# Sigmoid attention and a gated feed-forward network: the last four f chunks of batch 1 as a third unit of seven products

## The chip, the cores and the metric

The kernel runs on one core of one Trainium2 chip, in one launch. The metric is device time in microseconds; three runs of the kernel before gave 387.45, 387.88 and 389.07, a median of 387.88. One more execution was profiled.

Engines are named as in the profile: PE is TensorE (PEld its weight loads), DVE is VectorE, ACT is ScalarE, POOL is GpSimd, SP is SyncE.

## The reference

```python
# q, k, v: (8, 12, 448, 64) float32; w_gate, w_val: (768, 1536); w_out: (1536, 768)
scores = q @ k.T / sqrt(64) - log(448)
attn   = 1 / (1 + exp(-scores))                  # a sigmoid, no row sums
x      = (attn @ v), heads side by side          # (8 * 448, 768)
out    = (max(x @ w_gate, 0) * (x @ w_val)) @ w_out
```

## The kernel before

**Tiles.** All matmuls take 16-bit operands. A batch has 448 tokens and 12 heads; heads go in six pairs (the 768 model columns as six slices of 128), and three groups of four heads, g = 0, 1, 2. The 1536 hidden columns are twelve f chunks of 128. The 448 keys are seven chunks c of 64. A *scores unit* (b, g, c) (`qk_unit`) is eight matmuls of 64x64x448, four at a time in the four quadrants of TensorE, into two PSUM banks, and two sigmoids on ScalarE (L187) into a tile PT. A *PV* (`pv_group`) multiplies the seven PT tiles of a group by v into two banks, which VectorE empties into xT (L184). xT is x transposed, one tile a batch.

**PSUM.** Eight banks in a ring, `free`. `bank()` takes the next one; `later()` moves some to the back. A bank is written again when its reader is done.

**Feed-forward units.** For a plain chunk, `gv` makes gate and value products of one f chunk (twelve matmuls, L322), ScalarE or VectorE takes the positive part, VectorE multiplies into hT (L343). Batch 0 is done in two halves of 256 and 192 tokens (`push_first`, `ffn_mix`), between the scores of batch 1.

`gv_split(b, f)` (kind `"s"`) does four f chunks of one batch at once. It cuts the problem into 2x2 blocks (two halves of the model columns; gate and value weights; two halves of the tokens) and uses seven block products instead of eight, each twelve matmuls of 128x128x224 (L718). It needs sums of the weights: S3 = gate - value in place of half of the value weights (`gate_sums`), S2, S1, S4 (`unit_sum_steps`), each 128x768 on VectorE, for each pair of f chunks; and sums of the tokens T1, T2, T4, T3 (`split_sums`). From batch 2 on, two batches are taken together in the same scheme (`gv_pair`, kind `"w"`), with sums X of the tokens.

The last product with w_out is done in pairs of token tiles, `down_pair(g, p)` (kind `"y"`), seven products of six matmuls 128x128x384 (L389), with sums T of w_out (`weight_sums(i)`, 128x2304 each, one in place), sums S of hT (`token_sum_steps`), and results added up in `ysb`. For pairs in `SUMS_LATE` the product A12 x B21 comes second and has bank `a` of its own from the start; for others `a` is taken after the scores units that `amid` puts into the middle.

**Order.** It is written out by hand. `order` lists the 21 scores units of a batch; `cuts` cuts them into bursts, `pv_at` puts PVs into them. Batch b's loop runs burst, work, burst, work: for b = 1 the work is `ffn_mix(mix[m])` half-chunks of batch 0, from b = 2 on it is `next_work`, which pops the deque `work`. For b = 2 this is `("u", 1, 8), ("s", 1, 0), ("u", 1, 9), ("s", 1, 4), ("u", 1, 10), ("u", 1, 11)`, where `"u"` is a plain chunk of 448 tokens. `ahead` runs before a unit's matmuls are recorded, `jobs` in its middle (`beside`).

**Loads and transposes.** GpSimd issues all loads, in order; each issue waits until the one eight before it has landed. k and q of batch 0 and 1 are transposed on TensorE; from batch 2 on `dma_transposes(b, g)` copies k and q of a group into a tile `rel` (two 128x896 copies on VectorE, L222), and SP issues a DMA transpose into `qkT` (three buffers). `rel` has two buffers. `hold` is a copy on GpSimd that reads a transposed tile, so that the loads behind it (`late_loads`: v of batch 2, k and q of batch 3, w_out) wait for transpose (2, 1).

Of the kernel before, what the change touches and what calls it, by code (L numbers as in the profile page):

```python
# [18 lines left out]
def kernel(  # L19
# [75 lines left out]
    def tiles_of(b):  # L95
        if b not in in_tiles:
            pool = early if b == 1 else inp
# [58 lines left out]
    load(1, 1, 2, "kq")  # L156
    load_gv(6, 9)
    load_v(1)
    load(1, 2, 3, "kq")
    load_gv(9, 12)  # L160

# [55 lines left out]

    def dma_transposes(b, g):
        k16, q16, _ = in_tiles[b]
        rel = relp.tile([P, TW, P], FP16, tag="rel", name="rel")  # L220
        for ti, t16 in enumerate((k16, q16)):
            nc.vector.tensor_copy(  # L222
                rel[:, ti * NCH : (ti + 1) * NCH, :].rearrange("p c (h d) -> p h c d", h=2),
                t16[:, 2 * g : 2 * g + 2, :].rearrange("p h (c d) -> p h c d", c=NCH),
            )
        nc.sync.dma_start_transpose(
            qkT_of(b, g)[:], rel[:].rearrange("p c x -> p (c x)")
        )

    def row_of(r, hh):  # L230
# [139 lines left out]
    def open_late():  # L370
        first_sbuf.close()
        pool = ctx.enter_context(tc.tile_pool(name="late", bufs=1))
        T = pool.tile([P, 3, HF, HM], FP16, tag="T", name="T")
        late["T"] = [T[:, 0], T[:, 1], wo[:, 0:HF, HM:DM], T[:, 2]]
        late["odd"] = pool.tile([P, NFC, P], FP16, tag="odd", name="odd")
        late["X"] = pool.tile([P, 3, HD, S], FP16, tag="X", name="X")
        late["sums"] = ctx.enter_context(tc.tile_pool(name="sums", bufs=2))

    def sub(o, a, b):
# [26 lines left out]
    FRESH = {1: 0, 2: 0, 3: NPP}  # L406
    SUMS_LATE = {(1, 0), (1, 1), (2, 0), (2, 1), (3, NPP)}
    odd = {}
# [150 lines left out]

    def early_sum_steps(j, f):  # L560
        views = []
        for i in range(3 * j, 3 * j + 3):
            t = early.tile([P, 2, 512], FP16, tag=f"PT{i}", name="S")
            flat = t[:].rearrange("p a y -> p (a y)")[:, 0 : HD * 2 * P]
            views.append(flat.rearrange("p (x y) -> p x y", y=2 * P))
        yield lambda: gate_sums(f, f + 2)
        yield from unit_sum_steps(("s", f), f, views)

    def unit_sum_steps(key, f, tiles):
# [3 lines left out]
        S3, A22 = wv[:, 0:HD, fs], wv[:, HD:NDC, fs]  # L573
        sums[key] = S1, S2, S4
        return (
            lambda: sub(S2, A22, S3),
            lambda: nc.vector.tensor_tensor(out=S1, in0=S2, in1=A11, op=AOP.add),
            lambda: sub(S4, A12, S2),
        )

    def batch_blocks(g, ks):
        x1, x2 = xT_tiles[2 * g], xT_tiles[2 * g + 1]
        lo, hi = slice(*ks), slice(HD + ks[0], HD + ks[1])
        return [late["X"][:, i, lo] for i in range(3)] + [x1[:, lo], x1[:, hi], x2[:, lo], x2[:, hi]]

# [12 lines left out]
    def gv_pair(g, f, beside, first_copy):  # L598
        x1, x2 = xT_tiles[2 * g], xT_tiles[2 * g + 1]
        T1, T2, T4 = (late["X"][:, i] for i in range(3))  # L600
        B11, B21, T3, B22 = x1[:, 0:HD], x1[:, HD:NDC], x2[:, 0:HD], x2[:, HD:NDC]
# [82 lines left out]
    def split_sums(b):  # L684
        tile_ = xTp.tile([P, NPAIR, S], FP16, tag="xT", name="X2")
# [7 lines left out]
        sub(T1, B12, B11)  # L693
        sub(T2, B22, T1)
        sub(T4, B21, T2)
        sub(T3, B22, B12)

    def gv_split(b, f, beside):
# [8 lines left out]
        for j in range(4):  # L707
            us, fs = slice(j % 2 * P, (j % 2 + 1) * P), slice((f + j) * P, (f + j + 1) * P)
            S1, S2, S4 = (t[:, :, us] for t in sums[("s", f + j // 2 * 2)])
            sets.append((  # L710
                wg[:, 0:HD, fs], wg[:, HD:NDC, fs], wv[:, HD:NDC, fs],
                S1, S2, wv[:, 0:HD, fs], S4,
            ))
# [151 lines left out]

    def hold(b, g):
        nc.gpsimd.tensor_copy(gate[0:1, :], qkT_tiles[(b, g)][0:1, 0, 0:2])

# [39 lines left out]
    def next_work(jobs=(), alone=False, amid=None, ahead=()):  # L908
# [11 lines left out]
        if kind == "y":  # L920
            down_pair(g, i, beside, prepare, not work, scaled_act if alone else scaled, amid)
        elif amid:
# [11 lines left out]
    for b in range(1, B):  # L934
        if b == 1:
            cuts, pv_at = (0, 3, 6, 9, 13, 17, 21), {3: (0, 2), 5: (1, 2)}
        else:
            cuts, pv_at = (0, 4, 7, 11, 14, 18, 21), {0: (-1, 2), 2: (0, 2), 4: (1, 2)}
        bursts = list(range(len(cuts) - 1))
# [7 lines left out]
        if b == 1:  # L947
            mix = (4, 3, 3, 3, 3, 4)
            hooks = {
                1: [(3, lambda: both(1, 1))],  # L950
                3: [(3, lambda: both(1, 2))],
                4: [(2, lambda: dma_transposes(2, 0)), (0, lambda: dma_transposes(2, 1))],
                5: [(4, late_loads)],
            }
            steps = itertools.chain.from_iterable(early_sum_steps(j, 2 * j) for j in range(4))
            given = ((0, 0, 1, 1, 1), (0, 1, 1, 1), (0, 1, 1, 1), (0, 1, 1, 0), (2, 0, 0, 0), (0, 1, 1, 1, 0))
        else:
            mix = (0,) * count

        def burst(n):  # L960
            for i, (g, c) in enumerate(order[cuts[n] : cuts[n + 1]]):
# [9 lines left out]
                qk_unit(b, g, c)  # L971

        for m in range(count):
# [22 lines left out]
            if b == 2 and m == 0:  # L996
                ahead.append(lambda: split_sums(1))
            elif b == 2 and m == 4:
                open_late()
                first_sums = token_sum_steps(0, 0)  # L1000
                ahead += [*first_sums[:2], lambda: weight_sums(0)]
            elif b == 2 and m == 5:
                ahead += [lambda: weight_sums(1), lambda: dma_transposes(3, 2)]
                jobs += first_sums[2:]
            elif b == 3 and m == 0:
                jobs.append(lambda: (weight_sums(2), weight_sums(3)))
            elif b == 3:
                jobs.append(lambda: gate_sums(6 + 2 * m, 8 + 2 * m))
                if m == 1:
                    jobs.append(lambda: keep_odd(0))  # L1010
# [55 lines left out]
```

## Time and profile before

| | us |
|---|---|
| median of three runs | 387.88 |
| profiled execution | 388.3 |
| its span, first to last instruction | 386.5 |
| PE busy | 381.1 |
| DVE busy | 304.9 |
| ACT busy | 227.3 |
| POOL busy | 49.8 |
| granted TensorE clock, mean | 0.999 |

The page's second part gives the load of the DMA engines in 40 slices of 9.7 us; it is nine tenths or more in the first eleven slices and mostly lower after them. Matmuls are pipelined and a group's end is modelled, so durations of neighbours on PE overlap; the difference of two starts is what a group took.

Stages, from TensorE's order of time: first slots of batch 0 up to 29.70; batch 1's scores between batch 0's half-chunks up to 61.30; batch 2's scores between batch 1's feed-forward units up to 95.81; from there on batch 3's scores between the first pairs of the output product, in steps of 9.9 us.

### The profile page before, as it was taken

Reading aid. Unit: us, or ns where it says so; the run is one execution under the profiler, and the core shown is the slowest. Engines: PE = TensorE matmul, PEld = TensorE weight load, DVE = VectorE, ACT = ScalarE, POOL = GpSimd, SP = SyncE. Lnnn points to the kernel's source line nnn. Section 1 sums busy time; section 2 is a strip of 40 time slices with the busy share of each in tenths; the row PEclk is TensorE's granted clock in tenths of the full one; section 3 lists DMA queues with packets and bytes.
Section 4 is the critical chain, followed back from the end, with each engine's and each line's share of the span. In section 5 each row is a group of like instructions: output and inputs, shape, how many; then the busy total and the mean of one; then the engine's idle time right before and its main releaser. Section 6 shows DMA issues by size and latency. Waiting matters only on the chain.

```text
span 386.5 us, 8978 instructions
## 1 busy us (share of the span) xinstructions
PE 381.1 (99%) x3570; PEld 223.2 (58%) x3570; DVE 304.9 (79%) x611; ACT 227.3 (59%) x480; POOL 49.8 (13%) x73
## 2 busy tenths in 40 slices
PE   8999999999999999999999999999999999999996
PEld 6678776885555545455555554545455555555654
DVE  3455667769868999999868789999978788999653
ACT  5967887567777645455777764545477344333322
POOL 8643306100400003000300300000000000000000
PEclk9999999999999999999999999999999999999999
DMA  9999999999979302952499893222013220000235
GB/s 171 199 199 204 204 193 161 208 208 135 179 168 178 81 2 37 182 95 47 43 229 220 171 233 56 44 54 50 0 28 76 72 75 0 2 0 0 73 92 165
DMA packets 67563, 43.81 MB, mean 113 GB/s; under 512 B 35648, under 2 KB 64192, under 8 KB 67520
## 3 DMA queue, kind: packets, MB, share of 16 engines
q0 software_dynamic: 28960, 23.24, 39.2%
q1 hardware_dynamic: 37792, 19.34, 24.5%
q10 hardware_dynamic: 768, 0.66, 0.6%
q8 instruction: 28, 0.46, 0.5%
q14 instruction: 15, 0.12, 0.1%
HBM read 47.19 MB, written 11.01 MB: 151 GB/s over the span
## 4 chain that ended last, share of the span: by engine, by line
PE 96%; ACT 2%; DMA 1%; DVE 0%; issue 0%
PE u L389 34%; PE g L389 16%; PE y L389 12%; PE qk_ps L239 10%; PE pv_ps L257 8%; PE g_ps L322 5%; PE v_ps L322 5%; PE u L718 2%; PE g L718 2%; ACT PT L187 2%; DMA qkT<-rel 1%; PE warm_ps L175 1%; PE trt L204 1%; DVE ysb L544 0%; DVE zeros L130 0%
## 5 line engine op out<-in xcount | busy, mean ns | idle before, releaser
L187 ACT ACTIVATE PT<-qk_ps 128x448 f16<-128x448 f32 (+3 forms) x318 | 150.9, 584 | 79.2 <-PE qk_ps L239 79.1
L389 PEld LDWEIGHTS <-S 128*128 128x128 f16 x576 | 56.3, 98 | 45.9
L628 DVE TENSOR_TENSOR gsb<-g,gsb 128x448 f32<-128x448 f32 x72 | 42.7, 623 | 7.9 <-PE g L389 7.5
L239 PE MATMUL qk_ps<-qkT 64*64 64x448 f16 (+2 forms) x756 | 47.5, 337 | 0.7 <-DMA qkT<-rel 0.3
L389 PEld LDWEIGHTS <-hT 128*128 128x128 f16 x318 | 29.5, 98 | 24.0 <-issue 6.1
L257 PE MATMUL pv_ps<-PT,v 64*64 64x448 f16 (+2 forms) x756 | 36.6, 329 | 0.0
L468 DVE SCALAR_TENSOR_TENSOR ysb<-y,ysb 128x384 f32<-128x384 f32 x33 | 18.3, 555 | 20.7 <-PE y L389 14.1
L184 DVE TENSOR_SCALAR xT<-pv_ps 128x448 f16<-128x448 f32 (+2 forms) x53 | 27.8, 566 | 8.0 <-PE pv_ps L257 6.9
L389 PEld LDWEIGHTS <-wg 128*128 128x128 f16 x216 | 20.2, 98 | 21.8 <-issue 4.3
L389 PEld LDWEIGHTS <-wv 128*128 128x128 f16 x216 | 21.1, 98 | 19.7
L450 ACT ACTIVATE ysb<-u 128x384 f32<-128x384 f32 x28 | 13.8, 491 | 30.9 <-PE u L389 26.8
L389 PE MATMUL u<-wo,hT 128*128 128x384 f16 x156 | 29.8, 327 | 0.0
L239 PEld LDWEIGHTS <-qkT 64*64 64x64 f16 x756 | 17.6, 106 | 21.0 <-issue 14.1
L111 POOL DMA_DIRECT2D k<-in_k_dram x14 | 10.8, 775 | 141.0 <-DVE rel L222 135.9
L257 PEld LDWEIGHTS <-v 64*64 64x64 f16 x756 | 21.4, 107 | 11.1 <-issue 0.5
L389 PE MATMUL u<-xT,wg 128*128 128x448 f16 x108 | 23.5, 354 | 0.0
L389 PE MATMUL u<-xT,wv 128*128 128x448 f16 x108 | 23.4, 352 | 0.0
L389 PE MATMUL g<-X,S 128*128 128x448 f16 x108 | 23.4, 352 | 0.0
L389 PE MATMUL u<-X,S 128*128 128x448 f16 x108 | 23.4, 352 | 0.0
L389 PE MATMUL g<-xT,S 128*128 128x448 f16 x108 | 23.4, 352 | 0.0
L389 PE MATMUL g<-xT,wg 128*128 128x448 f16 x108 | 23.4, 352 | 0.0
L389 PE MATMUL u<-X,wv 128*128 128x448 f16 x108 | 23.4, 352 | 0.0
(98 smaller groups left out, 563.9 us busy)
## 6 DMA issues: line engine op xcount, KB each, us to landing
out_dram<-ysb SPq DMA_DIRECT2D x53, 192.0 KB, 3.1
v<-in_v_dram POOLq DMA_DIRECT2D x8, 336.0 KB, 15.3
v<-in_v_dram POOLq DMA_DIRECT2D x16, 168.0 KB, 15.1
k<-in_k_dram POOLq DMA_DIRECT2D x4, 672.0 KB, 11.6
q<-in_q_dram POOLq DMA_DIRECT2D x4, 672.0 KB, 14.8
wo<-in_moe_w_out_dram POOLq DMA_DIRECT2D x2, 1152.0 KB, 19.2
k<-in_k_dram POOLq DMA_DIRECT2D x9, 224.0 KB, 11.8
q<-in_q_dram POOLq DMA_DIRECT2D x7, 224.0 KB, 12.3
```

The source lines that it names most:

```text
L111: nc.gpsimd.dma_start(t16[:, xs, cs], rows_of(src, b)[:, xs, cs])
L175: nc.tensor.matmul(ps[:, 0:n], zeros[:, 0:P], zeros[:, 0:n], start=True, stop=True)
L184: nc.vector.tensor_scalar(out=xT, in0=src, scalar1=XSCALE, scalar2=None, op0=AOP.mult)
L187: nc.scalar.activation(PT_ap, ps_ap, AF.Sigmoid, bias=sig_bias, scale=qk_scale)
L239: nc.tensor.matmul(out_of(hh)[o : o + 64, :], qkT[rows, c, cols], qkT[rows, NCH + c0 : NCH + c1, cols], start=True, stop=True, tile_positi ...
L257: nc.tensor.matmul(ps[hh][64 * r : 64 * r + 64, 0:qn], v16[rows, 2 * g + hh, c * D : (c + 1) * D], pieces[c][rows, hh, :], start=(c == 0), ...
L322: nc.tensor.matmul(ps[:, 0:qn], (wg, wv)[i][:, dc, f * P : (f + 1) * P], xT_tiles[b][:, dc, q0 : q0 + qn], start=(dc == 0), stop=(dc == ND ...
L389: nc.tensor.matmul(ps[:, 0:n], A[:, k_, :], W[:, k_, :], start=(first and k_ == 0), stop=(k_ == kn - 1), skip_group_check=True,)
L450: nc.scalar.activation(o, ps[:, 0:HM], AF.Copy, scale=OUT_SCALE)
L468: nc.vector.scalar_tensor_tensor(out=o, in0=ps[:, 0:HM], scalar=OUT_SCALE, in1=o, op0=AOP.mult, op1=AOP.add)
L628: nc.vector.tensor_tensor(out=gs[u][i][:], in0=ps[u][:, 0:S], in1=gs[u][i][:], op=AOP.add)
L718: nc.tensor.matmul(ps[j // 2][:, j % 2 * SQ : (j % 2 + 1) * SQ], sets[j][i][:, k_, :], W[:, k_, :], start=(first and j % 2 == 0 and k_ == ...
```

## The change

Twelve f chunks of batch 1 are done as three units of seven products, f 0, 4 and 8, instead of two and four plain chunks. Chunks 10 and 11 of batch 0 are no longer done in halves beside batch 1's scores, but as plain chunks of 448 tokens beside batch 2's. Batch 2's scores go in five bursts of 5, 3, 5, 3, 5 units instead of six of 4, 3, 4, 3, 4, 3. The weight sums of f 8 to 11 are made in batch 2's stage into the four `ysb` buffers. For f 10 and 11 the difference S3 is written apart, so that the value weights stay; they are overwritten later, in batch 3. The weights of f 10 and 11 are loaded behind `hold`, in front of v of batch 2; those of f 9 in front of batch 2's k and q; v of batch 1 in front of the weights of f 6 to 8. Copies for transposes (3, 0) and (3, 1) run on ScalarE, those of (3, 2) move into batch 3. Pair (0, 0) joins `SUMS_LATE`, with its first copy on ScalarE; T2, T3, T4 of w_out and S4, S3 of the pair are made in batch 3's first step. Batch 1's k and q, the token sums X2 and later X live in a pool `mid`.

```diff
-    load_gv(6, 9)
     load_v(1)
+    load_gv(6, 9, (0,))
     load(1, 2, 3, "kq")
-    load_gv(9, 12)
+    load_gv(6, 9, (1,))
...
-    SUMS_LATE = {(1, 0), (1, 1), (2, 0), (2, 1), (3, NPP)}
+    SUMS_LATE = {(0, 0), (1, 0), (1, 1), (2, 0), (2, 1), (3, NPP)}
...
+    def output_views():
+        for _ in range(4):
+            t = ysbp.tile([P, 2, HD, 2 * P], FP16, tag="ysb", name="S")
+            yield t[:, 0]
+            yield t[:, 1]
+
+    def early_sum_steps(f, views, apart=False):
+        tiles = list(itertools.islice(views, 3))
+        fs = slice(f * P, (f + 2) * P)
+        S3 = next(views) if apart else wv[:, 0:HD, fs]
+        yield lambda: sub(S3, wg[:, 0:HD, fs], wv[:, 0:HD, fs])
+        yield from unit_sum_steps(("s", f), f, tiles, S3)
...
-    push_first(1, range(0, 4))
-    for f0 in range(4, 12, 2):
+    push_first(1, range(0, 3))
+    push_first(1, (3,), False)
+    by_vector = {(1, 3), (0, 5), (0, 6), (1, 6), (1, 7), (0, 9)}
+    for f0 in range(4, 10, 2):
         for half in range(2):
             for f in range(f0, f0 + 2):
-                push_first(half, (f,), (half, f) not in ((0, 9), (1, 8)))
+                push_first(half, (f,), (half, f) not in by_vector)
...
     def late_loads():
         dma_transposes(2, 2)
-        hold(2, 1)
+        hold(qkT_tiles[(2, 1)])
+        load_gv(10, 12)
         load_v(2)
-        load(3, 0, NG, "kq")
+        load(3, 0, 1, "kq")
+        load(3, 1, NG, "kq")
         load_o()
...
-            work.extend([("u", 1, 8), ("s", 1, 0), ("u", 1, 9), ("s", 1, 4), ("u", 1, 10), ("u", 1, 11)])
+            work.extend([("s", 1, 0), ("u", 0, 10), ("s", 1, 4), ("u", 0, 11), ("s", 1, 8)])
...
-            cuts, pv_at = (0, 4, 7, 11, 14, 18, 21), {0: (-1, 2), 2: (0, 2), 4: (1, 2)}
+            cuts = (0, 5, 8, 13, 16, 21) if b == 2 else (0, 4, 7, 11, 14, 18, 21)
+            pv_at = {0: (-1, 2), 2: (0, 2), 4: (1, 2)}
...
-            mix = (4, 3, 3, 3, 3, 4)
+            mix = (3, 2, 3, 2, 3, 3)
...
+                    load_gv(9, 10)
                     load(2, 0, 1, "kq")
...
+            if b == 2:
+                if m == 0:
+                    views = output_views()
+                    steps = itertools.chain.from_iterable(early_sum_steps(f, views, f == 10) for f in (8, 10))
+                    some = lambda n: [lambda: next(steps)()] * n
+                    ahead.append(of_tokens[1])
+                    jobs += [lambda: load_v(3), of_tokens[3], of_tokens[2], *some(2)]
+                elif m == 1:
+                    ahead += some(1)
+                elif m == 2:
+                    jobs += [*some(3), lambda: dma_transposes(3, 0, nc.scalar.copy)]
+                elif m == 3:
+                    open_late()
+                    first_sums = token_sum_steps(0, 0)
+                    ahead += some(2)
+                    jobs.append(first_sums[0])
+                else:
+                    jobs += [
+                        lambda: weight_sums(0), first_sums[1],
+                        lambda: dma_transposes(3, 1, nc.scalar.copy),
+                    ]
             elif b == 3 and m == 0:
-                jobs.append(lambda: (weight_sums(2), weight_sums(3)))
+                ahead.append(lambda: weight_sums(1))
+                jobs += [*first_sums[2:], lambda: weight_sums(2), lambda: weight_sums(3)]
+                jobs.append(lambda: dma_transposes(3, 2))
+            elif b == 3 and m == 1:
+                jobs += [lambda: keep_odd(0), lambda: gate_sums(10, 12)]
```

More of the change, by code (lines that the diff above doesn't have):

```diff
@@ L59 @@
     gsbp = ctx.enter_context(tc.tile_pool(name="gsbp", bufs=6))
+    mid = ctx.enter_context(tc.tile_pool(name="mid", bufs=1))
     first_sbuf = ExitStack()
@@ L96, in tiles_of @@
         if b not in in_tiles:
-            pool = early if b == 1 else inp
+            pool = mid if b == 1 else inp
             in_tiles[b] = tuple(
@@ L216, in transposed, with dma_transposes @@
         return copy
-    def dma_transposes(b, g):
+    def dma_transposes(b, g, copy=nc.vector.tensor_copy):
         k16, q16, _ = in_tiles[b]
@@ L221, in dma_transposes @@
         for ti, t16 in enumerate((k16, q16)):
-            nc.vector.tensor_copy(
+            copy(
                 rel[:, ti * NCH : (ti + 1) * NCH, :].rearrange("p c (h d) -> p h c d", h=2),
@@ L228, in dma_transposes @@
         )
+        return rel
     def row_of(r, hh):
@@ L375, in open_late, with open_X @@
         late["odd"] = pool.tile([P, NFC, P], FP16, tag="odd", name="odd")
-        late["X"] = pool.tile([P, 3, HD, S], FP16, tag="X", name="X")
         late["sums"] = ctx.enter_context(tc.tile_pool(name="sums", bufs=2))
+    def open_X():
+        k16, q16 = (mid.tile([P, NPAIR, S], FP16, tag=t, name="X") for t in ("k16", "q16"))
+        late["X"] = [k16[:, 0:HD], k16[:, HD:NDC], q16[:, 0:HD]]
     def sub(o, a, b):
@@ L558, in gate_sums, with early_views @@
         sub(wv[:, 0:HD, fs], wg[:, 0:HD, fs], wv[:, 0:HD, fs])
-    def early_sum_steps(j, f):
-        views = []
+    def early_views(j):
         for i in range(3 * j, 3 * j + 3):
@@ L564, in early_sum_steps, with unit_sum_steps @@
             flat = t[:].rearrange("p a y -> p (a y)")[:, 0 : HD * 2 * P]
[L565 to L569, printed above, removed]
+            yield flat.rearrange("p (x y) -> p x y", y=2 * P)
+    def output_views():
[9 more added lines that the diff above has]
+        yield from unit_sum_steps(("s", f), f, tiles, S3)
+    def unit_sum_steps(key, f, tiles, S3=None):
         S1, S2, S4 = tiles
@@ L572, in unit_sum_steps @@
         A11, A12 = wg[:, 0:HD, fs], wg[:, HD:NDC, fs]
-        S3, A22 = wv[:, 0:HD, fs], wv[:, HD:NDC, fs]
-        sums[key] = S1, S2, S4
+        S3 = wv[:, 0:HD, fs] if S3 is None else S3
+        A22 = wv[:, HD:NDC, fs]
+        sums[key] = (S1, S2, S4, S3) if key[0] == "s" else (S1, S2, S4)
         return (
@@ L583, in batch_blocks @@
         lo, hi = slice(*ks), slice(HD + ks[0], HD + ks[1])
-        return [late["X"][:, i, lo] for i in range(3)] + [x1[:, lo], x1[:, hi], x2[:, lo], x2[:, hi]]
+        return [late["X"][i][:, lo] for i in range(3)] + [x1[:, lo], x1[:, hi], x2[:, lo], x2[:, hi]]
     def batch_sums_t1(g):
@@ L599, in gv_pair @@
         x1, x2 = xT_tiles[2 * g], xT_tiles[2 * g + 1]
-        T1, T2, T4 = (late["X"][:, i] for i in range(3))
+        T1, T2, T4 = late["X"]
         B11, B21, T3, B22 = x1[:, 0:HD], x1[:, HD:NDC], x2[:, 0:HD], x2[:, HD:NDC]
@@ L684, in split_sums @@
     def split_sums(b):
-        tile_ = xTp.tile([P, NPAIR, S], FP16, tag="xT", name="X2")
+        tile_ = mid.tile([P, NPAIR, S], FP16, tag="k16", name="X2")
         flat = tile_[:].rearrange("p a s -> p (a s)")
@@ L692, in split_sums @@
         B11, B21, B12, B22 = x[:, 0:HD, 0:SQ], x[:, HD:NDC, 0:SQ], x[:, 0:HD, SQ:S], x[:, HD:NDC, SQ:S]
[L693 to L696, printed above, removed]
+        return (
+            lambda: sub(T1, B12, B11),
+            lambda: sub(T2, B22, T1),
+            lambda: sub(T4, B21, T2),
+            lambda: sub(T3, B22, B12),
+        )
     def gv_split(b, f, beside):
@@ L708, in gv_split @@
             us, fs = slice(j % 2 * P, (j % 2 + 1) * P), slice((f + j) * P, (f + j + 1) * P)
-            S1, S2, S4 = (t[:, :, us] for t in sums[("s", f + j // 2 * 2)])
+            S1, S2, S4, S3 = (t[:, :, us] for t in sums[("s", f + j // 2 * 2)])
             sets.append((
                 wg[:, 0:HD, fs], wg[:, HD:NDC, fs], wv[:, HD:NDC, fs],
-                S1, S2, wv[:, 0:HD, fs], S4,
+                S1, S2, S3, S4,
             ))
@@ L864, with hold @@
     open_banks("ring1")
-    def hold(b, g):
-        nc.gpsimd.tensor_copy(gate[0:1, :], qkT_tiles[(b, g)][0:1, 0, 0:2])
+    def hold(t):
+        nc.gpsimd.tensor_copy(gate[0:1, :], t[0:1, 0, 0:2])
     def both(b, g):
@@ L920, in next_work @@
         if kind == "y":
-            down_pair(g, i, beside, prepare, not work, scaled_act if alone else scaled, amid)
+            down_pair(g, i, beside, prepare, not work, scaled_act if alone or (g, i) == (0, 0) else scaled, amid)
         elif amid:
@@ L947 @@
         if b == 1:
-            mix = (4, 3, 3, 3, 3, 4)
+            mix = (3, 2, 3, 2, 3, 3)
             hooks = {
-                1: [(3, lambda: both(1, 1))],
-                3: [(3, lambda: both(1, 2))],
+                1: [(2, lambda: both(1, 1))],
+                3: [(2, lambda: both(1, 2))],
                 4: [(2, lambda: dma_transposes(2, 0)), (0, lambda: dma_transposes(2, 1))],
-                5: [(4, late_loads)],
+                5: [(3, late_loads)],
             }
-            steps = itertools.chain.from_iterable(early_sum_steps(j, 2 * j) for j in range(4))
-            given = ((0, 0, 1, 1, 1), (0, 1, 1, 1), (0, 1, 1, 1), (0, 1, 1, 0), (2, 0, 0, 0), (0, 1, 1, 1, 0))
+            steps = itertools.chain.from_iterable(early_sum_steps(2 * j, early_views(j)) for j in range(4))
+            given = ((0, 0, 2, 1), (0, 1, 1), (1, 1, 1, 1), (1, 1, 1), (0, 0, 1, 1), (1, 0, 1, 0))
         else:
@@ L971, in burst @@
                 qk_unit(b, g, c)
+        if b == 2:
+            of_tokens = split_sums(1)
+            of_tokens[0]()
         for m in range(count):
@@ L977 @@
                 jobs.append(lambda: dma_transposes(b, 2))
-            if b == 2 and m == 3:
-                jobs += [lambda: dma_transposes(3, 0), lambda: dma_transposes(3, 1)]
-            elif b == 3 and m == count - 1:
+            if b == 3 and m == count - 1:
                 jobs.append(lambda: dma_transposes(4, 1))
@@ L991 @@
                     load(2, 2, 3, "kq")
-            elif m == (2 if b == 4 else 0) and b + 1 < B:
+            elif b > 2 and m == (2 if b == 4 else 0) and b + 1 < B:
                 for g0, g1 in ((0, 1), (1, NG)) if b == 3 else ((0, NG),) if b > 3 else ():
@@ L995 @@
                 jobs.append(lambda: load_v(b + 1))
[L996 to L1004, printed above, removed]
-            elif b == 3 and m == 0:
-                jobs.append(lambda: (weight_sums(2), weight_sums(3)))
[L1007 to L1010, printed above, removed]
+            if b == 2:
+                if m == 0:
[18 more added lines that the diff above has]
+                    ]
+            elif b == 3 and m == 0:
+                ahead.append(lambda: weight_sums(1))
[3 more added lines that the diff above has]
+                jobs += [lambda: keep_odd(0), lambda: gate_sums(10, 12)]
             if b % 2 and b > 2:
                 if m == count - 1:
+                    if b == 3:
+                        open_X()
                     jobs.append(lambda: (batch_sums_t1(b // 2), batch_sums(b // 2, (0, 1))))
```

## The prediction

> **What bounds the kernel now.** I read the page first, then busy time by stage, TensorE's order of time, VectorE's and ScalarE's beside it, and the landings of single DMA issues.
>
> ```profile
> PE 381.1 (99%) x3570; PEld 223.2 (58%) x3570; DVE 304.9 (79%) x611; ACT 227.3 (59%) x480; POOL 49.8 (13%) x73
> PEclk9999999999999999999999999999999999999999
> 29.70:61.30 31.60, 31.60 (x428) 25.95 (x424) 21.11 (x52) 24.22 (x60) 7.99 (x12) 1.00 1.22 196
> 61.30:95.81 34.51, 34.51 (x385) 24.69 (x385) 26.45 (x49) 23.71 (x54) 6.76 (x10) 1.00 1.17 184
> 95.81:105.75 9.94, 9.94 (x101) 5.41 (x100) 7.78 (x13) 7.75 (x18) 4.95 (x7) 1.00 1.01 163
> ```
>
> The last three rows are the stages the change touches: batch 1's attention (29.70 to 61.30), batch 2's (61.30 to 95.81) and the first step of batch 3. Figures after the colon pair are length, then busy time of PE, PEld, DVE, ACT, POOL. TensorE is busy for the whole of each, at full clock. So removed matmul time is time won, and every wait put on TensorE is lost in full. TensorE in order of time (start, us):
>
> ```profile
> 56.60 0.83 PE L322 MATMUL g_ps<-xT,wg 128*128 128x256 f16 x6
> ...
> 59.23 0.66 PE L322 MATMUL g_ps<-xT,wg 128*128 128x192 f16 x6
> ...
> 61.30 0.57 PE L239 MATMUL qk_ps<-qkT 64*64 64x448 f16 x8
> 61.71 1.49 PE L257 MATMUL pv_ps<-PT,v 64*64 64x448 f16 x28
> 63.03 0.55 PE L239 MATMUL qk_ps<-qkT 64*64 64x448 f16 x8
> 63.51 1.31 PE L322 MATMUL g_ps<-xT,wg 128*128 128x448 f16 x6
> 64.66 1.30 PE L322 MATMUL v_ps<-xT,wv 128*128 128x448 f16 x6
> 65.88 0.76 PE L239 MATMUL qk_ps<-qkT 64*64 64x448 f16 x12
> 66.58 1.32 PE L718 MATMUL u<-xT,wg 128*128 128x224 f16 x12
> ...
> 74.73 0.57 PE L239 MATMUL qk_ps<-qkT 64*64 64x448 f16 x8
> ```
>
> Starts give prices: a long burst (four scores units around a PV) 2.21, a plain chunk of 448 tokens 2.37, a short burst (three units) 0.70, a unit of seven products 8.15. Check: 3x2.21 + 3x0.70 + 4x2.37 + 2x8.15 = 34.51, batch 2's stage exactly: it holds no wait.
>
> **The change, part by part.**
>
> *Matmuls.* Batch 1's stage loses four half-chunks of batch 0 (f 10 and 11): two of 256 tokens from 56.60 to 59.23 and two of 192 to 61.21: -4.61. Batch 2 then does two plain chunks and three units of seven in five bursts. A burst of five costs 2.21 + 0.20 (8 score matmuls start 0.41 apart from the PV, so 0.20 a unit): 3x2.41 + 2x0.70 + 2x2.37 + 3x8.15 = 37.82, against 34.51: +3.31. Together -1.30. That is the whole prize: 0.3% of the kernel.
>
> *Bursts of five.* Eight PSUM banks go round; a unit and a PV take two each, so the fifth unit falls on the second unit's banks.
>
> ```profile
> 61.73 3.60 ACT L187 ACTIVATE PT<-qk_ps 128x448 f16<-128x448 f32 x8 [0.48 <-PE qk_ps L239]
> ```
>
> Sigmoids start 0.43 into a burst, one every (3.60 - 0.565)/7 = 0.434, each 0.565 long: the fourth ends at 2.30. TensorE reaches the fifth unit at 1.73 + 2x0.20 = 2.13. About 0.17 is lost, three times: +0.5 (0 to 0.7).
>
> *Sums of weights and VectorE in batch 2.* Eight more sums at 0.47 apart (96.90 to 97.37), twelve more evictions of the third unit at 0.58, against what leaves: two products of plain chunks, six transpose copies, one 1.26 sum of w_out, two 0.47 sums. Net some +5.6, to 32.0 of 37.8. In a unit of seven starting at 2.6 after its burst, VectorE ends the addition that frees the first bank pair at 9.2; the seventh product's second half wants it at 10.1. Covered; no cover is left for more than 0.9. The difference kept apart (f 10) only changes an address; the tiles that change pool (token sums in batch 1's input tiles, weight sums in output buffers) have their last readers on TensorE before the next writer.
>
> *Two transpose copies moved to ScalarE.* VectorE does one in 0.385; ScalarE has no such row. Its nearest are 0.807 for 128x768 and 1.024 for 128x1024: I take 0.92 (0.385 to 1.024), 1.85 a pair. After a burst of five ScalarE ends ten sigmoids at 4.8, the unit's four copies at 6.85, and is next wanted at 11.2: hidden, with 2.5 to spare. [...]
>
> *Batch 3's first step.* Output pair (0, 0) now takes the order in which A12 x B21 comes second, in a bank of its own, ahead of the inner burst. Five products at 0.978 (98.02 to 99.00) end at 2.21 + 4.89 = 7.10; the inner burst starts at 7.19, and its third unit's second bank, reached at 7.62, is that very bank. VectorE empties it, but in VectorE's order seven things now stand before: two xT evictions, T2, S4, S3, T3, T4, the copies of transpose (3, 2).
>
> ```profile
> 97.84 1.15 DVE L184 TENSOR_SCALAR xT<-pv_ps 128x448 f16<-128x448 f32 x2
> 99.68 1.35 DVE L380 TENSOR_TENSOR wo<-wo 128x2304 f16<-128x2304 f16 x1
> 100.94 1.35 DVE L380 TENSOR_TENSOR T<-wo,T 128x2304 f16<-128x2304 f16 x1
> 102.21 0.55 DVE L468 SCALAR_TENSOR_TENSOR ysb<-y,ysb 128x384 f32<-128x384 f32 x1
> ```
>
> Evictions begin at 1.93 (0.20 behind the PV, as at 63.23), +1.08, +1.27 (T2), +0.47, +0.47, +1.26, +1.27, +0.60 (two copies at 0.30) = 8.35, +0.55 for the emptying: 8.90. TensorE waits from 7.62 to about 8.95: +1.3 (0 to 2.0). Next late would be the first copy of pair (0, 1); moved with TensorE it ends some 0.2 before its bank is wanted. Pair (0, 0)'s own first copy, now on ScalarE, ends at 4.5 behind eight sigmoids; the fourth product wants it at 5.1.
>
> *Loads, on POOL and SP.* Batch 2's stage now starts at 56.7, its second burst of five at 56.7 + 2.6 + 8.15 + 0.70 + 2.37 = 70.5, batch 3 at 95.0. Up to wv 6 to 8 as many bytes are queued as now up to batch 1's last q (issued 30.38, landing 12.7 later): 43.1, wanted at 44.6. Batch 2's k and q have 768 KB less ahead: of the 6.3 that wg and wv 9 to 11 (1152 KB) take now, 4.2; their copies come some 3.5 earlier. The hold waits for transpose (2, 1): copied by 52.1, landing 4.4 after its issue (as at 55.82): 56.6 instead of 60.2. Behind it on POOL stand wg and wv 10, 11, then v of batch 2, k and q of batch 3, w_out. Now v's three loads land at 67.5 to 68.6, 7.9 after the first issue at 60.73, of which 3.3 is their own traffic. Then: first issue 57.1, + 4.6 + 2x2.0 for the weights = 65.7 (wv wanted at 69.3), + 3.3 = 69.0 for v, wanted by the PV at 71.0. Bounds: 67 to 73. Transpose (3, 0) issues at 70.5 + 6.85 + 1.85 = 79.2; among the same loads it takes 10.95 now (82.66 to 93.61): 90.2, wanted at 95.0. SP's order stays: the three transposes, then pair (0, 0)'s stores, which are ready only after (3, 2) has issued. The load of batch 4 waits for the copies of (3, 2): issue 103.4 instead of 95.97, last q 12.2 later as now: 115.6, wanted at 120. None of these is charged.
>
> *Sum.* -1.30 + 0.5 + 1.3 = +0.5 on the profiled execution's 388.3 (span 386.5 and 1.8 around it) = 388.8. The runs' median, 387.88, lies 0.4 below it: 388.4.
>
> **Rivals.**
>
> *The cover holds: 386.6 to 387.2.* If VectorE empties the bank in time, only the bursts' 0 to 0.5 is lost: 387.88 - 1.30 + 0 to 0.6. For it: VectorE has 2.16 idle in that step now. Against: the work put there is 1.27 + 0.94 + 0.60 more, in front. Chance 0.15.
>
> *Batch 2's values come late: slower.* The weights went ahead of v on POOL, and the PV comes 4.4 earlier. The margin is 2.0; from a landing at 71.0 on, TensorE waits in full. At a landing of 72.5 to 73.5 the sum is 388.4 + 1.5 to 2.5 = 389.9 to 390.9. For it: the 4.6 of start-up was measured once, beside one transpose. Against: fewer loads are then in flight. Chance 0.16.
>
> *ScalarE's copies, or transpose (3, 0) behind them, come late.* Copies of over 2.2 each would delay the next sigmoids; a landing over 15.8 after its issue would delay batch 3: 389.4 to 391. The longest transpose up to there took 10.95 now. Chance 0.07.
>
> *Weight loads show.* The change has 12 matmuls more, so 12 more 98 ns weight loads; if each stood in the open, +1.2: 389.6. Against: twelve 224-column matmuls start 1.15 apart, 96 ns each, so their loads are hidden. [...] Chance 0.02.
>
> **How the numbers follow.** The forecast (387.4 to 389.4 with its bounds) has 0.58, something unseen 0.02. About 0.5% (1.9 us) is what a measurement of this kernel can tell from no change: faster means below 385.9, slower above 389.8. No mechanism here reaches below 386.5, so faster keeps 0.04, for what I have not seen. Slower: 0.13 of late values, 0.05 of late copies, 0.03 of the forecast's upper tail: 0.21. Same: 0.75. The range runs from the first rival's lower end to late values, 386.6 to 390.8.
>
> **What would show it.** Right: batch 2's first burst at about 56.7 and its stage at 37.8 to 38.5; batch 3's first step at about 11.2 instead of 9.94, with the inner burst's last unit waiting for ysb<-y on VectorE; transpose copies of 0.9 on ScalarE. Wrong: a step of 9.94 there; PV of batch 2 waiting for v; any wait of TensorE behind 126 us that is not there now.

## The result, and the profile after

The changed kernel takes 391.64 us (median of six runs, 391.44 to 392.84) against 388.00 for the kernel before on the same chip: 1.0096 of it, interval 1.0080 to 1.0112. The profiled execution took 391.44, with a span of 389.6 (before: 388.3 and 386.5). The kernel is slower, and above the upper end of the forecast's range.

The page's line of busy times and its line of the granted clock:

```profile
PE 380.6 (98%) x3582; PEld 225.8 (58%) x3582; DVE 313.4 (80%) x625; ACT 229.4 (59%) x478; POOL 52.4 (13%) x77
PEclk9999999999999999999999999999999999999999
```

The table by stage; the five rows are batch 1's attention, batch 2's, and the three steps of batch 3, with figures as in the prediction: length, then PE, PEld, DVE, ACT, POOL.

```profile
29.25:56.86 27.61, 27.20 (x382) 21.86 (x378) 19.89 (x48) 21.69 (x52) 7.45 (x10) 1.00 1.27 190
56.86:96.22 39.36, 38.93 (x445) 31.55 (x444) 33.38 (x62) 28.74 (x60) 10.43 (x15) 1.00 1.15 179
96.22:107.54 11.32, 10.31 (x100) 5.51 (x99) 11.12 (x19) 7.75 (x17) 2.66 (x4) 1.00 0.44 53
107.54:117.47 9.93, 9.93 (x99) 5.40 (x98) 6.27 (x13) 7.30 (x16) 2.29 (x4) 1.00 1.24 221
117.47:128.71 11.24, 10.01 (x101) 5.41 (x100) 9.41 (x21) 8.18 (x18) 0.00 (x0) 1.00 1.22 210
```

TensorE is busy 0.5 us less than before and the clock is full, so all that was lost is waiting. Before, length and PE busy were equal in every one of these stages; now four of the five hold a gap. The second and third steps of batch 3 took 9.93 each before. By stage the change cost -3.99, +4.85, +1.38, 0, +1.31: together +3.55, close to the 3.64 between the medians. (The span grew by only 3.1, since this execution reached its first half-chunk 0.45 earlier, at 29.25 instead of 29.70. In the traces below that moment lies between 29.1 and 30.2, so stages are compared, not moments.)

From the waits of TensorE (us in total, times, longest), the lines that belong to the lost time:

```profile
PE qk_ps L241 <- DMA qkT<-rel: 1.2, 1, 1.2
...
PE qk_ps L241 <- DVE ysb L473: 1.0, 1, 1.0
PE trt L205 <- DVE hT L345: 0.4, 1, 0.4
...
PE qk_ps L241 <- DVE gate_sb L338: 0.2, 1, 0.2
...
PE qk_ps L241 <- DVE hT L345: 0.2, 1, 0.2
```

And where they stand in TensorE's order of time:

```profile
34.01 0.58 PE L205 MATMUL trt<-ident,q 128*64 128x128 f16 x14 [0.41 <-DVE hT L345]
...
57.45 0.35 PE L241 MATMUL qk_ps<-qkT 64*64 64x448 f16 x1 [0.21 <-DVE gate_sb L338]
57.97 0.38 PE L241 MATMUL qk_ps<-qkT 64*64 64x448 f16 x3 [0.18 <-DVE hT L345]
...
105.17 0.38 PE L241 MATMUL qk_ps<-qkT 64*64 64x448 f16 x3 [1.01 <-DVE ysb L473]
...
128.71 0.57 PE L241 MATMUL qk_ps<-qkT 64*64 64x448 f16 x8 [1.23 <-DMA qkT<-rel]
```

Four places, and only the third was forecast. They are called here by what is late.

*The half-chunk's bank* (34.01). In batch 1's first gap two sums of weights stand on VectorE ahead of hT of the third half-chunk; the transposes of q of (1, 1) want the bank that this hT frees. VectorE's order of time there, two sums and then the eviction:

```profile
32.55 0.55 DVE L385 TENSOR_TENSOR wv<-wg,wv 128x768 f16<-128x768 f16 x1
33.14 0.56 DVE L385 TENSOR_TENSOR S<-wv 128x768 f16<-128x768 f16 x1
33.62 0.34 DVE L345 TENSOR_TENSOR hT<-gate_sb,v_ps 128x192 f16<-128x192 f32 x1
```

*The rel buffer* (57.45 and 57.97). VectorE's order of time just before batch 2's first burst:

```profile
55.90 0.39 DVE L223 COPY rel<-k 128x896 f16<-128x896 f16 x1 [1.55 <-DMA qkT<-rel]
56.21 0.39 DVE L223 COPY rel<-q 128x896 f16<-128x896 f16 x1
56.51 0.55 DVE L593 TENSOR_TENSOR S<-S,wg 128x768 f16<-128x768 f16 x1
56.98 0.41 DVE L338 TENSOR_SCALAR gate_sb<-g_ps 128x256 f32<-128x256 f32 x1
57.50 0.69 DVE L345 TENSOR_TENSOR hT<-gate_sb,v_ps 128x256 f16<-128x256 f32 x2
```

The copies for transpose (2, 2) want the rel buffer that transpose (2, 0) is still reading. VectorE stands 1.55 us, and behind it in its order stand the evictions of batch 0's last three half-chunks, whose banks the burst wants. The burst takes 3.49 (56.86 to 60.35); the other two bursts of five take 2.64. The row was there in the kernel before as well, shorter and with no cost:

```profile
58.38 0.40 DVE L222 COPY rel<-k 128x896 f16<-128x896 f16 x1 [0.91 <-DMA qkT<-rel]
```

*The bank of A12 x B21* (105.17), the forecast one. VectorE in batch 3's first step: T3, T4 and the copies of transpose (3, 2) end just before the addition that empties it:

```profile
101.43 1.35 DVE L385 TENSOR_TENSOR wo<-wo 128x2304 f16<-128x2304 f16 x1
102.70 1.35 DVE L385 TENSOR_TENSOR T<-wo,T 128x2304 f16<-128x2304 f16 x1
103.97 0.38 DVE L223 COPY rel<-k 128x896 f16<-128x896 f16 x1
104.27 0.38 DVE L223 COPY rel<-q 128x896 f16<-128x896 f16 x1
104.57 1.01 DVE L473 SCALAR_TENSOR_TENSOR ysb<-y,ysb 128x384 f32<-128x384 f32 x2
```

*Transpose (4, 0)* (128.71), wanted by batch 4's first burst. GpSimd's order of time gives the first load of batch 4, and the DMA view of the one transpose issued at 119.95 its time to landing:

```profile
104.88 0.74 POOL L112 DMA_DIRECT2D k<-in_k_dram  x1 [32.80 <-ACT PT L188]
```

```profile
qkT<-rel SPq DMA_TRANSPOSE x1, 8.7
```

Before, that load was issued at 95.97 and the transpose took 6.3 and landed 1.15 ahead of its demand. Now the load is issued 8.9 later, behind the copies of (3, 2), its last part lands at 125.51, and the transpose among that traffic lands at 128.66. (GpSimd's row names a sigmoid as what it waited for; the copies of (3, 2) on VectorE end at 104.65, just before the issue.) The four stores that SP issues just ahead of the transpose take longer too: 5.2 to 6.5 from issue to landing, before 2.6 to 3.9.

### The profile page after: what moved, and what is told of

Read it like the earlier page. It is cut to its first block, busy times and chain, and to the rows that moved or that the text cites. A ratio compares the mean times of both kernels' runs of the same rounds, so it can differ in the third digit from the quotient of the medians.

```text
span 389.6 us, 9013 instructions
## 1 busy us (share of the span) xinstructions
PE 380.6 (98%) x3582; PEld 225.8 (58%) x3582; DVE 313.4 (80%) x625; ACT 229.4 (59%) x478; POOL 52.4 (13%) x77
## 4 chain that ended last, share of the span: by engine, by line
PE 89%; DMA 5%; DVE 3%; ACT 2%; issue 1%; DVEq 0%; ACTq 0%
PE u L394 33%; PE g L394 16%; PE y L394 11%; PE qk_ps L241 9%; PE pv_ps L259 8%; DMA qkT<-rel 4%; PE u L736 4%; PE g_ps L324 3%; PE v_ps L324 3%; PE g L736 3%; ACT PT L188 2%; DMA ysb<-in_k_dram 1%; PE trt L205 1%; DVE T L385 1%; DVE rel L223 0%
## 5 line engine op out<-in xcount | busy, mean ns | idle before, releaser
L241 PE MATMUL qk_ps<-qkT 64*64 64x448 f16 (+2 forms) x756 | 48.6, 336 | 3.2 <-DMA qkT<-rel 1.2
L241 PEld LDWEIGHTS <-qkT 64*64 64x64 f16 x756 | 18.8, 105 | 24.2 <-issue 16.4
```

The source lines that it names most:

```text
L241: nc.tensor.matmul(out_of(hh)[o : o + 64, :], qkT[rows, c, cols], qkT[rows, NCH + c0 : NCH + c1, cols], start=True, stop=True, tile_positi ...
```

## The experiments

Four kernels take one wait each out of the changed kernel; two put a cause to the test from the other side; four are combinations. All stage lengths are from their traces, in the order of the table above.

**Transpose (4, 0).** One job moves to the front of its list:

```diff
-                jobs += [*first_sums[2:], lambda: weight_sums(2), lambda: weight_sums(3)]
                 jobs.append(lambda: dma_transposes(3, 2))
+                jobs += [*first_sums[2:], lambda: weight_sums(2), lambda: weight_sums(3)]
```

> In batch 3's first step the two copies for transpose (3, 2) go ahead of S4, S3, T3 and T4 on VectorE, so the load of batch 4 should issue at about 101.1 instead of 104.88. The theory (four separate waits of TensorE, one of them set by this load): the loads end some 3.7 earlier, transpose (4, 0) then lands at about 126 to 127.3 instead of 128.66, the third step of batch 3 goes from 11.24 back to 9.93 to 10.3, the other steps stay (the first at 11.3, as its sum of work is the same), and the whole is about 1.0 to 1.3 shorter: 390.3 to 390.7. First rival (the stores of the output pairs, which also run beside transpose (4, 0), make it late): third step still 11.0 to 11.3, whole 391.4 to 391.7. Second rival (VectorE simply has too much work there): the time moves to another wait, whole unchanged.

390.94 us, 1.0072 of before (1.0048 to 1.0096). The first and third steps of batch 3:

```profile
96.50:107.82 11.32, 10.31 (x100) 5.50 (x99) 11.12 (x19) 7.75 (x17) 4.95 (x7) 1.00 0.70 99
...
117.75:127.69 9.94, 9.94 (x100) 5.41 (x100) 8.24 (x19) 7.69 (x17) 0.00 (x0) 1.00 1.01 191
```

The load is issued at 101.69, the transpose takes 6.1 instead of 8.7, and the third step has no wait. The sum of the five stages falls from 99.46 to 98.19. Both rivals fall: the stores follow the same products, which run 0.28 later than in the changed kernel (the third step starts at 117.75 instead of 117.47), and no other wait takes the place. The stores may belong to the chain, as a link and not as the cause: with the load earlier, the median of all 53 stores from issue to landing is 3.4 instead of 3.8. The median lies 0.2 above the range expected, and its interval overlaps the changed kernel's (1.0080 to 1.0112), so what one wait is worth is read from the stages, here and below.

The same cause put into the kernel *before*, by itself:

```diff
-                ahead += [lambda: weight_sums(1), lambda: dma_transposes(3, 2)]
+                ahead += [lambda: weight_sums(1)]
...
                 jobs.append(lambda: (weight_sums(2), weight_sums(3)))
+                jobs.append(lambda: dma_transposes(3, 2))
```

> The kernel before with one thing of the change: the two copies for transpose (3, 2) run in batch 3's first step behind T3 and T4 on VectorE, so the load of batch 4 issues at about 102.8 instead of 95.97. The theory (transpose (4, 0) lands when that load lets it, about 23.8 behind its first issue as in the changed kernel): it lands at about 126.3 instead of 124.46, 0.7 behind its demand at 125.61, so the third step of batch 3 takes 10.4 to 10.9 instead of 9.93, the rest stays, and the whole is 0.4 to 1.0 longer than the kernel before. Rival (the lateness in the changed kernel came from its later stores): third step 9.93, no difference.

388.88 us, 1.0021 of before (1.0011 to 1.0031). The load and batch 4's first burst:

```profile
102.76 0.74 POOL L111 DMA_DIRECT2D k<-in_k_dram  x1 [34.20 <-DVE rel L222]
```

```profile
126.01 0.57 PE L239 MATMUL qk_ps<-qkT 64*64 64x448 f16 x8 [0.46 <-DMA qkT<-rel]
```

A wait of 0.46 (third step 10.47) appears where the kernel before had 1.15 in hand, from nothing but two copies issued 6.8 later. So the later copies alone make the wait (transpose (3, 2) moves with them; in the changed kernel it had landed at 112.61, 7.3 ahead of the issue of (4, 0)); its size is at the lower end, since the load came 2.1 earlier than in the changed kernel. Of the 0.93 between the medians the third step shows 0.54; the rest is not in the stages of the one execution that was profiled.

**The bank of A12 x B21.** T1 one unit earlier, T2 in T1's place:

```diff
-                    ahead += some(2)
+                    ahead += [*some(2), lambda: weight_sums(0)]
...
-                        lambda: weight_sums(0), first_sums[1],
+                        lambda: weight_sums(1), first_sums[1],
...
-                ahead.append(lambda: weight_sums(1))
```

> T1 of w_out is made one unit earlier in batch 2's stage and T2 takes T1's old place, so that 1.27 of VectorE's work leaves batch 3's first step. The theory: y1 += A12 x B21 starts at about 103.3 instead of 104.57, the bank is free before the inner burst's third unit wants it at 104.16, the 1.01 of waiting goes and the first step takes about 10.3 instead of 11.32; the load of batch 4 issues 1.27 earlier, so the third step's wait stays at about 1.0 to 1.3; whole 390.3 to 390.7. Rival (the wait for transpose (4, 0) takes over whatever is won ahead of it): first step 10.3, third step 12.2, whole 391.4 to 391.7. Second rival (VectorE is the bound of batch 2's stage): that stage grows from 39.36 to about 40.6 and the whole stays.

391.05 us, 1.0088 of before (1.0056 to 1.0119), above the 390.3 to 390.7 expected. In the trace the five stages take 27.61, 39.73, 10.10, 9.93 and 11.19, together 98.56 instead of 99.46.

```profile
96.84:106.94 10.10, 10.10 (x100) 5.51 (x100) 10.04 (x18) 7.45 (x17) 2.66 (x4) 1.00 0.31 60
```

The wait of 1.01 is gone and the step lost 1.22 of its length, as the theory says; the third step did not grow to 12.2, so the first rival falls. The load of batch 4 moves with the end of the step (four of its seven issues fall into the step in both kernels, POOL 2.66), the step is 1.2 shorter, and the wait for transpose (4, 0) stays (1.19). Batch 2's stage is 0.37 longer, but not through the sums: 0.36 of it is its first burst (0.57 waited for gate_sb instead of 0.21); what made that wait longer was not shown.

**The rel buffer.** The copies of (2, 2) behind two of the three half-chunks:

```diff
-                5: [(3, late_loads)],
+                5: [(1, late_loads)],
```

> Only the place of the two copies for transpose (2, 2) on VectorE changes: behind the second of the last three half-chunks of batch 0 instead of ahead of the first. The theory (VectorE stood 1.55 for a rel buffer with the evictions of the last half-chunks queued behind): the copies find the buffer free at about 56, batch 2's first burst takes 2.6 to 2.7 instead of 3.49, its stage 38.5 instead of 39.36, whole about 0.85 shorter in the trace (span 388.7). Rival (a burst of five units at the start of the ring costs 3.5 whatever VectorE does): first burst still 3.4 to 3.5, span 389.6.

One execution: 392.61 us, no shorter than the changed kernel (391.44 to 392.84); the five stages sum to 100.18 instead of 99.46. The first burst took 2.64 (57.31 to 59.95), as the theory has it; the copies found their buffer free. But what was won there was lost again, and more, at two transposes:

```profile
96.85 0.57 PE L241 MATMUL qk_ps<-qkT 64*64 64x448 f16 x8 [0.94 <-DMA qkT<-rel]
...
129.88 0.57 PE L241 MATMUL qk_ps<-qkT 64*64 64x448 f16 x8 [1.78 <-DMA qkT<-rel]
```

The first is new: transpose (3, 0), issued at 79.76, landed only at 96.81.

```profile
qkT<-rel SPq DMA_TRANSPOSE x1, 17.0
```

So the theory was right on the burst and wrong on the whole: a further late piece lay 1.6 us behind the first.

**Why transpose (3, 0) takes 17 us.** In that kernel, v of batch 3 is loaded only when the transpose has landed:

```diff
-                    jobs += [lambda: load_v(3), of_tokens[3], of_tokens[2], *some(2)]
+                    jobs += [of_tokens[3], of_tokens[2], *some(2)]
...
-                    jobs.append(first_sums[0])
+                    jobs += [first_sums[0], lambda: (hold(qkT_tiles[(3, 0)]), load_v(3))]
```

> The kernel with the copies of (2, 2) moved, and in it v of batch 3 is loaded only when transpose (3, 0) has landed (a second hold). Theory (the transpose waits for the loads that run beside it): with 1.3 MB less beside it, it lands 3 or more earlier, at 91 to 94 instead of 96.81, batch 3's first burst no longer waits 0.94, and batch 2's stage takes 38.6 instead of 39.5. Rival (the transpose is slow by itself among any loads): it lands at 96 to 97 as without the hold.

The DMA view of that one transpose, and batch 2's stage:

```profile
qkT<-rel SPq DMA_TRANSPOSE x1, 12.0
```

```profile
57.11:95.63 38.52, 38.52 (x445) 30.86 (x444) 32.33 (x59) 28.62 (x60) 10.62 (x16) 1.00 1.07 166
```

It landed at 91.52, 5.3 earlier, and the stage holds no wait. (390.97 us, one execution.) The rival falls.

**The half-chunk's bank.**

```diff
-            given = ((0, 0, 2, 1), (0, 1, 1), (1, 1, 1, 1), (1, 1, 1), (0, 0, 1, 1), (1, 0, 1, 0))
+            given = ((0, 0, 0, 3), (0, 1, 1), (1, 1, 1, 1), (1, 1, 1), (0, 0, 1, 1), (1, 0, 1, 0))
```

> Two of the three sums of weights in batch 1's first gap move behind the last half-chunk's eviction on VectorE (0, 0, 0, 3 in place of 0, 0, 2, 1). The theory: hT of that half-chunk is written at about 32.55 instead of 33.62, the transposes of q of (1, 1) on TensorE no longer wait 0.5 for its bank, batch 1's stage takes about 27.1 instead of 27.61, span about 389.1. Rival (the bank is late for another reason, or the sums then hold the copies of the transposes and the wait comes at the next unit): stage 27.6, span 389.6.

One execution: 392.15 us, again no shorter. Batch 1's stage took 27.00 (30.16 to 57.16) instead of 27.61, and the transposes of q follow those of k with no wait:

```profile
33.92 0.58 PE L205 MATMUL trt<-ident,k 128*64 128x128 f16 x14
34.34 0.56 PE L205 MATMUL trt<-ident,q 128*64 128x128 f16 x14
```

The span was 390.4 and not 389.1: this execution began batch 1's stage 0.91 later than the changed kernel's, behind a weight load (TensorE waited 0.6 for wv there), and 0.26 of what was won went into a longer first burst (57.16 to 60.91, 3.75 instead of 3.49), with 0.45 waited for gate_sb instead of 0.21. The rival falls by the stage; the whole does not show the gain.

**All four edits together.**

> All four edits together. Batch 1's stage 27.0, batch 2's first burst 2.64, first step of batch 3 10.1, third step 9.93. Theory as it stands after the run with the copies of (2, 2) moved (transpose (3, 0) lands when the loads behind hold end, whenever TensorE wants it): the 0.6 and 0.85 won ahead of batch 3 are lost again where batch 3's first burst waits for transpose (3, 0), some 0.9 to 1.6, so batch 3 starts about 67 behind batch 1's first half-chunk, as in the changed kernel; only the two waits behind it are won for good: 2.3 less than the changed kernel, 389.0 to 389.5. Rival (transpose (3, 0) lands a fixed time behind its own issue): it comes 1.4 earlier too, and the whole is 387.3 to 387.8.

388.62 us, 1.0013 of before (1.0001 to 1.0025). The first three stages:

```profile
29.12:56.11 26.99, 26.99 (x380) 21.76 (x376) 20.88 (x51) 21.68 (x52) 7.46 (x10) 1.00 1.32 193
56.11:95.57 39.46, 38.60 (x445) 30.86 (x444) 33.72 (x61) 28.62 (x60) 10.45 (x15) 1.00 1.17 181
95.57:105.62 10.05, 10.05 (x98) 5.51 (x98) 9.36 (x17) 7.40 (x17) 4.95 (x7) 1.00 0.76 106
```

One wait is left, 0.87 at batch 3's first burst for transpose (3, 0), which again took 17.0. As expected it eats the 0.84 won at the first burst; the rival, a fixed time from issue to landing, falls. The median lies 0.4 below the expected range: batch 3 started 66.45 behind the first half-chunk, where the changed kernel has 66.97, so most of the 0.6 of batch 1 stayed won.

**With v of batch 3 held as well,** and f 11's weights loaded behind v and the first k and q:

```diff
-        load_gv(10, 12)
+        load_gv(10, 11)
         load_v(2)
         load(3, 0, 1, "kq")
+        load_gv(11, 12)
```

> The four edits, v of batch 3 held behind transpose (3, 0), and the weights of f 11 loaded behind v and the first k and q instead of ahead of v. The theory: no wait but the known ones is left from batch 1 to batch 4: 27.0 + 38.5 + 10.1 + 9.93 + 9.93 = 95.46 from the first half-chunk of batch 1's stage to batch 4's first burst, against 95.90 in the kernel before and 99.46 in the changed one: 387.2 to 387.8, 0.998 to 1.000 of the kernel before. Rival (there is always another late load): one more wait of 0.5 to 1.5 shows, for v of batch 2, v of batch 3 or transpose (3, 1), and the whole is 388 to 389.

388.08 us, 1.0002 of before (0.9991 to 1.0013), above the 387.2 to 387.8 expected.

```profile
29.23:56.22 26.99, 26.99 (x380) 21.77 (x376) 20.89 (x51) 21.68 (x52) 7.46 (x10) 1.00 1.32 193
56.22:94.80 38.58, 38.58 (x446) 30.87 (x445) 32.50 (x59) 28.62 (x60) 12.48 (x18) 1.00 1.11 163
94.80:105.26 10.46, 10.30 (x100) 5.55 (x100) 10.39 (x19) 7.69 (x17) 4.95 (x7) 1.00 1.37 164
```

The five stages sum to 95.89, against 95.91 in the kernel before. TensorE waits for no DMA any more, so the rival falls; which of the two edits v of batch 3 and the weights of f 11 needed was not taken apart here (the run with v held alone lost its wait for transpose (3, 0) too). The first step of batch 3 is 0.36 above what was expected: here the copies of (3, 2) stand in front and batch 3 starts earlier, so VectorE comes to the addition only at 102.28 and is late for the bank again (the step is 0.53 over 9.93; as a wait the trace shows 0.15 of it).

**T4 behind the addition,** in that kernel:

```diff
             plus(y1[:, lo], a)
+            if (g, p) == (0, 0):
+                weight_sums(3)
             product(c, S1, T1)
...
-                jobs += [*first_sums[2:], lambda: weight_sums(2), lambda: weight_sums(3)]
+                jobs += [*first_sums[2:], lambda: weight_sums(2)]
```

> The kernel with the four edits, values held and weights of f 11 behind, and in it T4 of w_out is made behind y1 += A12 x B21 on VectorE instead of ahead of it. The theory: the bank of A12 x B21 is read at about 101 instead of 102.28, so the remaining 0.5 of batch 3's first step goes (10.46 to 9.93 to 10.0), T4 is ready at 103.4 and wanted at 103.7; from batch 1's first half-chunk to batch 4's first burst 95.4 instead of 95.89, against 95.90 in the kernel before: 0.998 to 1.000 of it, 387.3 to 387.8. Rival (T4 now comes late for the last product of the pair): the first step stays at 10.2 to 10.5 and the whole at 1.000.

388.18 us beside 388.29 for the kernel before on the same chip: 0.9993 (0.9984 to 1.0002). It has the lowest ratio of all and is not measurably faster than before; the 387.3 to 387.8 expected were not reached, though the first step took 9.93 as expected and the rival falls. The trace:

```profile
29.43:56.43 27.00, 27.00 (x381) 21.77 (x378) 20.88 (x51) 21.68 (x52) 7.28 (x10) 1.00 1.28 191
56.43:94.95 38.52, 38.52 (x445) 30.86 (x445) 32.89 (x60) 28.62 (x60) 12.33 (x18) 1.00 1.10 164
94.95:104.88 9.93, 9.93 (x99) 5.40 (x98) 9.89 (x18) 7.28 (x17) 4.95 (x7) 1.00 1.38 150
```

From the first half-chunk to batch 3 this is 65.52 against 66.11 before, with no wait in either: 0.59 is all that the change's matmuls are worth once the longer bursts are paid. This profiled execution (389.21, the longest of its eleven) shows one more thing: in the three steps of batch 3 the DMA engines moved 150, 209 and 198 GB/s, in the run before 164, 236 and 211, and transpose (4, 0) came 1.59 late. Why they moved less in that execution stays open, and so does how many of the eleven had it: one was profiled. (In the run with fewer long bursts, the same kernel from there on, the three steps took 9.93, 9.93 and 9.94 and TensorE waited for no transpose.)

**Fewer long bursts.**

```diff
-            cuts = (0, 5, 8, 13, 16, 21) if b == 2 else (0, 4, 7, 11, 14, 18, 21)
+            cuts = (0, 5, 9, 13, 17, 21) if b == 2 else (0, 4, 7, 11, 14, 18, 21)
...
-            pv_at = {0: (-1, 2), 2: (0, 2), 4: (1, 2)}
+            pv_at = {0: (-1, 2), 2: (0, 2), 4: (1, 1 if b == 2 else 2)}
```

> As the run with T4 behind, with batch 2's scores cut into bursts of 5, 4, 4, 4, 4 instead of 5, 3, 5, 3, 5. The theory (a burst of five with a PV loses 0.23 for ScalarE's pace, a burst of four, with a PV or without, nothing): 2.64 + 1.02 + 2.21 + 1.02 + 2.21 = 9.10 instead of 3 x 2.64 + 2 x 0.69 = 9.30, the stage 38.3 to 38.4 instead of 38.58, the whole 0.2 shorter. Rival (a PV one unit earlier in its burst waits for the sigmoid of its last PT tile, or the fuller bursts without PV hold ScalarE's copies back): the stage 38.6 or longer.

388.16 us, 1.0004 (0.9984 to 1.0025). The theory falls, and the stage is in the rival's range: the five bursts took 2.64, 1.09, 2.44, 1.10 and 2.83, together 10.10, and the stage 39.29. The last burst ended in a wait of the unit behind it for the PV's eviction:

```profile
87.36 1.31 PE L738 MATMUL u<-xT,wg 128*128 128x224 f16 x12 [0.53 <-DVE xT L185]
```

A burst of four with a PV is not free here either (2.44 where the kernel before has 2.21).

## Why the prediction was wrong

It forecast +0.5 (-1.30 of matmuls, +0.5 of bursts, +1.3 of a bank); the stages show +3.55.

*Matmuls, -1.30: right.* Without the waits, batch 1's stage takes 27.00 instead of 31.60 (-4.60, forecast -4.61). Batch 2's takes 38.52: 37.82 as summed, plus the bursts.

*Bursts of five, +0.5: the size a little low.* 2.64 instead of 2.41, so 0.23 each and 0.69 for three. ScalarE's ten sigmoids in such a burst:

```profile
85.85 4.47 ACT L188 ACTIVATE PT<-qk_ps 128x448 f16<-128x448 f32 x10
```

*The bank of A12 x B21, +1.3: right.* 1.38, at the unit and for the reason given; the addition came 8.35 behind the step's start, as worked out. VectorE's busy time in batch 2's stage came out at 33.4 instead of 32.0, at no cost.

*ScalarE's copies, at no cost: right.* They took 0.94 each (forecast 0.92) and ScalarE stood idle 2.67 behind them. Weight loads did not show: at 98 ns each, as before, the products of a unit of seven still start 1.15 apart for twelve matmuls (61.50, 62.65, 63.80). And v of batch 2 landed at 70.07 (forecast 69.0), 1.9 ahead of its PV.

*"None of these is charged": the step that failed, at batch 4's load.* The text had the load at 103.4, its last q at 115.6, wanted at 120, and stopped there. That is the demand of the copies, and the copies were on time. The load was issued at 104.88 and its last q landed 15.0 later, at 119.86, not 12.2 later; v of batch 4, behind it, landed at 125.51. The transpose behind the copies runs beside what is left of that load and beside the stores, which took 5.2 to 6.5 instead of 2.6 to 3.9, and it had only 1.15 in hand before the change. So a term was put at nothing that measured 1.31, shown by the two kernels that move that one pair of copies. The prediction's own sign for being wrong, a wait of TensorE behind 126 us, is the one that came.

*The same paragraph, at the rel buffer.* "their copies come some 3.5 earlier" and "landing 4.4 after its issue" were used to date the hold behind (2, 1); what VectorE does while (2, 0) is under way was not asked, though the trace of before shows it standing 0.91 for that very buffer. Transpose (2, 0) took 5.69 instead of 4.65, one half-chunk fewer lies behind it as cover, and a burst of five follows. Cost 0.84. Why it took 1.04 longer stays open: the last load ahead of it had landed at 51.95, 1.8 behind its issue, where before it was 56.11, 2.5 behind.

*Batch 1's stage, not looked at.* It was priced by its matmuls alone. The sums of weights had been dealt out anew among the shorter gaps (`given`, which the diff of the change does not show: the first gap went from (0, 0, 1, 1, 1) to (0, 0, 2, 1)), and the first gap got two ahead of an eviction. Cost 0.61.

*Transpose (3, 0), at no cost: right by luck.* Forecast to land at 90.2 with 4.8 in hand; it landed at 94.62 with 1.6. It was taken to last as long as before from its issue. It does not: it ends with the loads (below). The kernel without the rel wait shows that 1.6 was all the cover there was.

Missing in the sum: 1.31 + 0.84 + 0.61 + 0.19 + 0.08 = 3.03 of the 3.05 between 0.5 and 3.55 (transpose (4, 0), the rel buffer, the half-chunk's bank, the bursts, the bank of A12 x B21). Rival "values late" had the right kind of fault, a DMA with less in hand, at the wrong transfer.

## What to carry to other kernels

In a kernel whose bound engine never waits, a change that shortens a stage spends the margin of every transfer and buffer that the stage covered: list for each the landing, the demand and what is in hand (here 1.15, 1.6 and 1.9 us), and compare them with the time won. Follow a delayed load to its last consumer, through copy and transpose, and not only to its first. An idle time of an engine off the path, when it stands in front of evictions that the bound engine's banks hang on, is a wait that is about to show (here VectorE's 0.91 before the change, 0.84 on TensorE after it).

## What the runs showed of the hardware

A DMA transpose's time to landing went with the traffic beside it. Each moves 448 KB (14 x 128 x 128 of two bytes), and yet in the changed kernel they took 3.9 at least and 14.5 at most, in others up to 17.0. Transpose (3, 0) landed 1.0 behind the last load issued before it in the kernel before (93.61 against 92.58) and 0.7 behind it in the changed one (94.62 against 93.95); with v held it took 12.0 instead of 17.0. An issue that came earlier gained nothing while the loads stayed: with the four edits it was issued 1.6 earlier than in the changed kernel, took 17.0 instead of 14.5 and landed at 95.53 instead of 94.62.

The packets show how the two shared the engines. The changed kernel from 84 to 88, with transpose (3, 0) and loads both under way; q0 carries GpSimd's loads, q1 what SP issues, then packets, MB and the share of the 16 engines:

```profile
q0 software_dynamic: 505, 0.66, 92.7%
q1 hardware_dynamic: 506, 0.13, 24.2%
```

One packet went for one (506 against 505), but a load's packet held 1.3 KB on average and the transpose's 0.26, so the transpose moved a fifth of what the loads moved. The counts do not show the order on one engine.

Loads and stores issued behind a transpose seem to hold it back as well: transpose (3, 2) of the changed kernel had nothing under way ahead of it at 104.73, seven loads were issued behind it on the other queue and four stores on its own, and it took 7.9. Transpose (4, 0) landed 3.15 and 3.33 behind the last of the loads and stores ahead of it (changed: 128.66 against 125.51; before: 124.46 against 121.13).

Without such traffic a transpose still took 4.8: (3, 1) of the changed kernel, issued at 94.06, had no load, store or other transpose beside it from 94.62 on and landed at 99.45. From 94.7 to 99.4:

```profile
q1 hardware_dynamic: 1824, 0.46, 97.8%
```
